# A convolution feeding a multiplicative FFN: block 3 transposed by DMA, and the first quarter of block 4 stored and transposed ahead of the rest

## The chip, the cores and the metric

The kernel runs on one core of a Trainium2 chip. The metric is device time in microseconds (us), one execution at a time; the profile is of one execution. The engines are named as the profile names them: PE (matmuls), ACT, DVE, POOL, and SP, which here only issues DMAs.

## The reference

A causal depthwise convolution with 7 taps per head (the softmax of `weight`, 8 heads of 24 channels), then a feed-forward block whose two input products are multiplied element by element and which has two linear layers behind that.

```python
w = softmax(weight, axis=-1)                          # 8 x 7
x_pad = concat([zeros(8, 6, 192), x], axis=1)         # x: 8 x 3904 x 192
t = einsum('hk,bskhg->bshg', w, windows(x_pad, 7))    # -> 31232 x 192
a, b = t @ w1, t @ w2                                 # 192 x 1024 each
out = ((a * b) @ w3) @ w_out                          # 1024 x 1024, 1024 x 192
```

## The kernel before

The 31232 tokens are handled as two streams of 15616 (`NS = 2`) in the two halves of the partitions. A stream is cut into windows of 58 tokens (64 rows with the 6 rows of padding), and the 272 windows are grouped into blocks of 10, 8, 10, 8, six of 36, and 20 windows. A *round* R is 512 tokens of both streams, so blocks 0 to 3 (2088 tokens) cover rounds 0 to 3 (2048 tokens), and block 4 (windows 36 to 71) covers rounds 4 to 7.

- `load_x(b)` brings a block's windows in from POOL's DMA queue with a cast (L112). `zero(b)` (L501) then clears the padding of windows at the start of a sequence; POOL waits there for the load.
- `conv(b, h0, nh, evict)` is the convolution as matmuls with a band matrix (L278); ACT or DVE copies the result from PSUM into `convo` (L295).
- The second product needs no transposing, the first does: `xT` holds the convolved rows with channels on partitions, in a ring of four rounds. Blocks 0 to 3 get there on PE, `pe_transposes(b)` (L331, copied out by ACT, DVE, ACT at L343). Later blocks go to a DRAM tile `rows` with `store(b)` (L322, L316; two DMAs a piece, of 48 and of 10 partitions, issued by SP), and come back by `transposes(R)`, three DMA transposes of 512 rows x 128 channels (L351, SP). The counters `stored` and `sent` tell `send(last)` which rounds may go.
- `first_product(R, between)` runs eight steps `ft`; each has 2 x 6 matmuls (L378) into two of four pairs of PSUM banks; ACT copies one to `asb` (L384), DVE multiplies it with the other into `abT` (L385). `between` puts convolutions and PE transposes behind given steps.
- `second_product(R, r)` (L404, L409) multiplies `abT` by `W_sb` and stores the result (L416; from POOL's queue in the first group, from SP's later).
- `W_sb` is w3 @ w_out, made on the chip: `load_w3` copies w3 to DRAM in bf16 in two halves (L430) and brings it back transposed with 16 DMA transposes on SP (L433), eight for each half of its rows; `w3_product(jt)` (L440) is eight matmuls over `gt`, and jt 0 to 3 read the first half of `w3T`, jt 4 to 7 the second.
- `P(out=pace, in_=w3T...)` (L472) makes POOL wait for one of these transposes before it issues the loads of blocks 4 and 5.

The order is written out by hand. First come rounds 0 to 3, with block R+1 convolved and transposed by PE inside round R for R = 0, 1, 2. Then `w3_product`, then the second products of rounds 0 to 3 with the convolution of block 4 (three slots of heads) and of block 5 between them. Then groups of four rounds follow: four first products, eight second products with the next block's convolution.

```python
    first_product(0, {
        3: seq((conv, 1, 0, 4)),
        5: seq((conv, 1, 4, 4)),
        6: seq((pe_transposes, 1))})
    for R in (1, 2):
        first_product(R, {
            0: seq((conv, R + 1, 0, 4)),
            2: seq((conv, R + 1, 4, 4)),
            5: seq((pe_transposes, R + 1))})
    store(3, FIRST[4] - 1)
    first_product(3)
```

Every engine runs its instructions in order, and each DMA issued by SP first waits for the DMA that was issued eight before it.

Of the kernel before, what the change touches and what calls it, by code (L numbers as in the profile page):

```python
# [16 lines left out]
def kernel(  # L17
# [10 lines left out]
    nc = tc.nc  # L28
# [4 lines left out]
    DFF = moe_w1.shape[1]  # L33
    JT = DFF // 128
# [3 lines left out]
    TS = B * S // NS  # L38
    CH = 512
    NR = -(-TS // CH)  # L40
    GROUP = 4
    RING = GROUP * CH
    Q = 64
    ST = Q - PAD
    NP = D // Q
    WB = -(-S // ST)
    NWIN = (B // NS) * WB
    LAST = S - (WB - 1) * ST
    SIZES = [10, 8, 10, 8] + [36] * 6 + [20]
    assert sum(SIZES) == NWIN  # L50
    NB = len(SIZES)
    FIRST = [sum(SIZES[:b]) for b in range(NB)]
# [3 lines left out]
    def tok(i):  # L56
        return (i // WB) * S + (i % WB) * ST
# [26 lines left out]
    rows = dram.tile([TS, NP * NS * Q], BF16, name="rows")  # L84


    def halves_of(b):
        n = SIZES[b] // 2
        return [(FIRST[b], 2 * n)] if 2 * n <= MAXN else [(FIRST[b], n), (FIRST[b] + n, n)]
# [8 lines left out]
    def load_x(b, parts=(0, 1)):  # L98
        tiles = xb_of.setdefault(b, [])
        zeros_of = zero_rows.setdefault(b, [])  # L100
        for i0, n in [v for e, v in enumerate(halves_of(b)) if e in parts]:
            xb = work.tile([128, n, D], BF16, tag="xb", bufs=5, name="xb")
            w = 0
            while w < n:
                i = i0 + w
                m = min(n - w, WB - i % WB)
                at_end = i + m == NWIN
                if at_end:
                    m -= 1
                if m:  # L110
                    for r in range(NS):
                        nc.gpsimd.dma_start(out=xb[Q * r:Q * r + Q, w:w + m, :],  # L112
                                            in_=x_spans(r, i, m))
                if i % WB == 0:
                    zeros_of += [(xb, 0, w), (xb, 1, w)]
                w += m
                if at_end:
                    nc.gpsimd.memset(xb[Q:128, w, :], 0.0)
                    t = tok(NWIN - 1) - PAD
                    nc.gpsimd.dma_start(out=xb[0:Q, w, :], in_=x_rows[t:t + Q, :])  # L120
                    nc.gpsimd.dma_start(out=xb[Q:Q + PAD + LAST, w, :],
                                        in_=x_rows[TS + t:TS + t + PAD + LAST, :])
                    w += 1
            if len(halves_of(b)) == 1:
                tiles += [(xb, 0), (xb, SIZES[b] // 2)]
            else:
                tiles.append((xb, 0))
# [8 lines left out]
    pace = const.tile([1, 2], BF16)  # L136
# [31 lines left out]
    for p0 in (0, Q):  # L168
        nc.gpsimd.affine_select(  # L169
            out=diag[p0:p0 + Q], in_=ones[p0:p0 + Q].to_broadcast([Q, Q + PAD]),  # L170
# [3 lines left out]
    for r in range(NS):  # L174
        nc.gpsimd.dma_start(out=xb0[Q * r + PAD:Q * r + Q, 0, :],
                            in_=x_rows[r * TS:r * TS + ST, :])
# [13 lines left out]
    def warm(n, t=None):  # L190
# [16 lines left out]
        out=wall, in0=wall, in1=wmax.unsqueeze(2).to_broadcast([1, H, K]), op=ALU.subtract)  # L207
# [6 lines left out]
        out=wrow, in0=wall, in1=wsum.unsqueeze(2).to_broadcast([1, H, K]), op=ALU.mult)  # L214
# [80 lines left out]
            f[e % len(f)](out=dst, in_=part)  # L295
        drained(p)

    stored, sent = [0], [GROUP]

    def store(b, first=0, queue=nc.sync):  # L300
        stored[0] = tok(FIRST[b] + SIZES[b]) if b + 1 < NB else TS
        n = SIZES[b] // 2
        convo = convo_of[b]
        for c in range(2):
            w = 0
            while w < n:
                i = FIRST[b] + c * n + w
                if i < first:
                    w += 1
                    continue  # L310
                left = WB - 1 - i % WB
                src = convo[Q * c:Q * c + ST, w:w + max(1, min(n - w, left))]
                src = src.rearrange("s w k r g -> s w (k r g)")
                j0 = tok(i)
                if left == 0:
                    queue.dma_start(out=rows[j0:j0 + LAST, :], in_=src[0:LAST, 0, :])  # L316
                    w += 1
                    continue
                m = min(n - w, left)
                dst = rows[j0:j0 + ST * m, :].rearrange("(w s) c -> s w c", s=ST)  # L320
                for s0, s1 in ((0, 48), (48, ST)):
                    queue.dma_start(out=dst[s0:s1], in_=src[s0:s1])  # L322
                w += m

    def pe_transpose(b, k):
# [36 lines left out]
    def width(R):  # L362
        return min(CH, TS - R * CH)

    def first_product(R, between=None):
        N = width(R)
        ab = work.tile([128, JT, NS, CH], BF16, tag="abT", bufs=GROUP, name="abT")
        abT_of[R] = ab
        r0 = (R * CH) % RING
        for ft in range(JT):  # L370
            pq = []
            for i in range(2):
                q, p = banks()
                pq.append((q, p))
                for k in range(NP):
                    for r in range(NS):
                        rs = slice(Q * r, Q * r + Q)
                        nc.tensor.matmul(  # L378
                            p[:, r, 0:N], wd[i][rs, k, ft * 128:(ft + 1) * 128],
                            xT[k][rs, r0:r0 + N],  # L380
                            start=(k == 0), stop=(k == NP - 1))
            (qa, pa), (qb, pb) = pq
            asb = work.tile([128, NS, CH], BF16, tag="asb", bufs=3, name="asb")
            nc.scalar.copy(out=asb[:, :, 0:N], in_=pa[:, :, 0:N])  # L384
            nc.vector.tensor_tensor(out=ab[:, ft, :, 0:N], in0=asb[:, :, 0:N],  # L385
                                    in1=pb[:, :, 0:N], op=ALU.mult)
            drained(qa)
            drained(qb)
            if between and ft in between:
                between[ft]()  # L390
# [34 lines left out]
    w3T = const.tile([128, JT, DFF], BF16)  # L425
    w3rows = dram.tile([DFF, DFF], BF16, name="w3rows")

    def load_w3():
        for j in range(0, DFF, CH):
            nc.gpsimd.dma_start(out=w3rows[j:j + CH], in_=moe_w3[j:j + CH])  # L430
        for j in range(0, DFF, CH):
            for gt in range(JT):
                nc.sync.dma_start_transpose(  # L433
                    out=w3T[:, gt, j:j + CH],
                    in_=w3rows[j:j + CH, gt * 128:(gt + 1) * 128])

    def w3_product(jt):
        p, wps = banks()
# [7 lines left out]
    V, A, P = nc.vector.tensor_copy, nc.scalar.copy, nc.gpsimd.tensor_copy  # L446
# [22 lines left out]
            copy_w(part, i, f)  # L469
    load_w3()  # L470
    nc.gpsimd.dma_start(out=wo_b, in_=wor)
    P(out=pace, in_=w3T[0:1, 1, DFF - 2:DFF])  # L472
    load_x(4)
    load_x(5)

    def seq(*fs):
        def run():
            for f, *a in fs:
                f(*a)
        return run  # L480

    def send(last):
        while sent[0] <= min(last, NR - 1) and min((sent[0] + 1) * CH, TS) <= stored[0]:
            transposes(sent[0])
            sent[0] += 1
# [2 lines left out]
        3: seq((conv, 1, 0, 4)),  # L488
        5: seq((conv, 1, 4, 4)),
        6: seq((pe_transposes, 1))})  # L490
    for R in (1, 2):
        first_product(R, {
            0: seq((conv, R + 1, 0, 4)),
            2: seq((conv, R + 1, 4, 4)),
            5: seq((pe_transposes, R + 1))})
    store(3, FIRST[4] - 1)
    first_product(3)

    def zero(b):
        for xb, r, w in zero_rows.pop(b, []):  # L500
            nc.gpsimd.memset(xb[Q * r:Q * r + PAD, w, :], 0.0)  # L501

    def conv_heads(b, heads, f=(nc.vector.tensor_copy,)):
        for j, h in enumerate(heads):
            conv(b, h, 1, (f[j % len(f)],))
        if heads[-1] == H - 1:
            store(b)

    slots = (range(0, 3), range(3, 6), range(6, H))
    zero(4)  # L510
# [6 lines left out]
    for p, rounds in enumerate(groups):  # L517
        b = PROLOGUE_BLOCKS + p
        order = rounds[-1:] + rounds[:-1] if rounds[-1] == NR - 1 else rounds
        for j, R in enumerate(order if p else ()):  # L520
            first_product(R)
            send(R + GROUP)
            if j < 2 and b < NB:
                P(out=pace, in_=abT_of[R][0:1, JT - 1, 1, 0:2])  # L524
                load_x(b, (j,))
        if b < NB:
            zero(b)
        at = {1: [(b, slots[0])], 3: [(b, slots[1])], 5: [(b, slots[2])]}
        if p == 0:
            at = {0: [(4, slots[1], (V, A))], 1: [(4, slots[2], (V, A))],  # L530
                  3: at[1], 5: at[3], 6: at[5]}
        for i, (R, r) in enumerate((R, r) for R in rounds for r in range(NS)):
            second_product(R, r, R == NR - 1 and r == 1, nc.sync if p else nc.gpsimd)
            for c in at.get(i, ()) if b < NB else ():
                conv_heads(*c)
            if p == 0 and i == 1:
                send(2 * GROUP - 1)
# [31 lines left out]
```

## Time and profile before

| | |
|---|---|
| median of 3 runs | 529.07 us (528.61 to 530.71) |
| the profiled execution | 530.22 us, of which the span from first to last instruction is 528.3 us |
| PE busy | 516.0 us, 98% |
| DVE, ACT busy | 359.1 us (68%), 325.0 us (62%) |
| round 0 starts on PE | 10.6 us |
| `w3_product` starts on PE | 60.0 us |
| last second product of rounds 0 to 3 ends | 90.9 us |
| matmuls of round 4 without pauses from | 96.6 us |
| a group of four first products later on | 41.55 us |

The span is the time between the first and the last instruction of the profile; the execution's own time has about 1.9 us around it. The busy time of PE is modelled for pipelined matmuls. The chain of waits follows the work that ended last back through what released it.

### The profile page before, as it was taken

What the parts mean: (1) busy time and instruction counts of PE and PEld (TensorE: products, weight loads), DVE (VectorE), ACT (ScalarE), POOL (GpSimd) and SP (SyncE); (2) the same over time, 40 slices, a digit from 0 to 9 for tenths busy, and PEclk for the clock granted to TensorE, in tenths of its full rate; (3) what the DMA queues carried; (4) which work ended last, traced back from release to release, by engine and by line L of the source; (5) the groups of instructions that cost most, each with busy time, mean ns of one, the idle gap of its engine ahead of it and who ended that gap; (6) DMA issues with size and microseconds to landing.
All of it is one profiled execution on the core that took longest, in us unless ns stands there. A gap on an engine that the chain in (4) does not pass through costs nothing.

```text
span 528.3 us, 12785 instructions
## 1 busy us (share of the span) xinstructions
PE 516.0 (98%) x5464; PEld 342.1 (65%) x5464; DVE 359.1 (68%) x347; ACT 325.0 (62%) x411; POOL 55.5 (10%) x93
## 2 busy tenths in 40 slices
PE   7999998799999999999999999999999999999997
PEld 4555787355786557965579555795558945599667
DVE  6777645499655996559964699637994289921880
ACT  5888642377536775367753777437774377744762
POOL 8405112012000110001200020000200000000000
PEclk9999999799999999999999999999999999999999
DMA  9999969699548793487834889347783631024004
GB/s 128 202 153 142 188 130 206 164 168 136 94 136 195 114 121 66 144 186 113 118 83 131 177 119 109 91 138 175 90 67 91 170 97 41 17 91 150 2 1 150
DMA packets 133381, 64.59 MB, mean 122 GB/s; under 512 B 90234, under 2 KB 132620, under 8 KB 133260
## 3 DMA queue, kind: packets, MB, share of 16 engines
q1 hardware_dynamic: 94378, 44.10, 37.2%
q0 software_dynamic: 38800, 19.58, 30.7%
q8 instruction: 42, 0.69, 0.5%
q14 instruction: 15, 0.12, 0.1%
q10 hardware_dynamic: 146, 0.10, 0.1%
HBM read 33.25 MB, written 36.52 MB: 132 GB/s over the span
## 4 chain that ended last, share of the span: by engine, by line
PE 93%; DMA 2%; DVE 2%; ACT 2%; issue 0%; POOL 0%; SPq 0%; POOLq 0%; ACTq 0%
PE pairs L378 58%; PE pairs L404 31%; PE pairs L278 2%; DVE abT L385 2%; ACT asb L384 1%; DMA xT<-rows 1%; PE pairs L440 1%; DMA xb<-in_x_dram 1%; PE pairs L331 1%; POOL xb L165 0%; DVE convo L449 0%; ACT xT L449 0%; ACT xT L343 0%; POOL diag L169 0%; ACT convo L295 0%
## 5 line engine op out<-in xcount | busy, mean ns | idle before, releaser
L385 DVE TENSOR_TENSOR abT<-asb,pairs 128x1024 bf16<-128x1024 bf16 (+1 forms) x248 | 298.4, 1204 | 83.1 <-ACT asb L384 44.6
L378 PE MATMUL pairs<-xT,wd 64*128 64x512 bf16 (+1 forms) x2976 | 322.5, 374 | 5.8 <-DMA xT<-rows 4.8
L384 ACT CAST asb<-pairs 128x1024 bf16<-128x1024 f32 (+1 forms) x248 | 247.6, 998 | 75.8 <-PE pairs L378 73.6
L378 PEld LDWEIGHTS <-wd 64*128 64x128 bf16 x2976 | 164.5, 94 | 157.9 <-issue 8.0
L404 PEld LDWEIGHTS <-abT 128*128 128x128 bf16 x1952 | 159.6, 98 | 9.7 <-issue 9.7
L404 PE MATMUL pairs<-W_sb,abT 128*128 128x192 bf16 x1952 | 165.9, 246 | 0.0
L409 ACT COPY osb<-pairs 128x384 f32<-128x384 f32 x122 | 58.3, 478 | 115.8 <-PE pairs L404 115.8
L295 DVE CAST convo<-pairs 128x864 bf16<-128x864 f32 (+5 forms) x67 | 50.8, 814 | 67.3 <-PE pairs L278 67.3
L112 POOL DMA_DIRECT2D xb<-in_x_dram x40 | 30.9, 791 | 7.9 <-PE pairs L378 4.6
L524 POOL COPY pace<-abT 1x2 bf16<-1x2 bf16 x10 | 1.7, 174 | 247.9 <-DVE abT L385 247.9
L278 PE MATMUL pairs<-xb,Aband 64*64 64x432 bf16 (+3 forms) x352 | 16.6, 294 | 1.0 <-DMA xb<-in_x_dram 1.0
L278 PEld LDWEIGHTS <-Aband 64*64 64x64 bf16 x352 | 6.6, 105 | 7.9 <-issue 6.9
L416 POOL DMA_DIRECT2D out_dram<-osb x8 | 6.1, 758 | 26.8 <-ACT osb L409 26.8
L295 ACT CAST convo<-pairs 128x512 bf16<-128x512 f32 (+4 forms) x15 | 8.1, 584 | 0.3 <-PE pairs L278 0.2
L409 DVE COPY osb<-pairs 128x192 f32<-128x192 f32 x1 | 0.4, 358 | 11.1 <-PE pairs L404 11.1
L440 PEld LDWEIGHTS <-w3T 128*128 128x128 bf16 x64 | 5.2, 98 | 0.4 <-issue 0.4
L440 PE MATMUL pairs<-wo_b,w3T 128*128 128x192 bf16 x64 | 5.5, 246 | 0.0
L195 PE MATMUL pairs<-zeros 128*128 128x512 bf16 x8 | 3.7, 595 | 1.3 <-DVE zeros L145 1.3
L331 PE MATMUL pairs<-identw,convo 128*128 128x128 bf16 x54 | 4.2, 219 | 0.7 <-DVE convo L449 0.6
L331 PEld LDWEIGHTS <-convo 128*128 128x128 bf16 x54 | 3.2, 97 | 2.5 <-issue 1.5
L442 ACT CAST W_sb<-pairs 128x192 bf16<-128x192 f32 x8 | 2.6, 319 | 2.8 <-PE pairs L440 2.8
L501 POOL MEMSET xb<- 6x192 bf16 x6 | 1.5, 250 | 21.7 <-DMA xb<-in_x_dram 21.7
(51 smaller groups left out, 40.6 us busy)
## 6 DMA issues: line engine op xcount, KB each, us to landing
out_dram<-osb SPq DMA_DIRECT2D x52, 384.0 KB
xb<-in_x_dram POOLq DMA_DIRECT2D x18, 432.0 KB, 8.6
rows<-convo SPq DMA_DIRECT2D x9, 648.0 KB
out_dram<-osb POOLq DMA_DIRECT2D x8, 384.0 KB, 6.7
w3rows<-in_moe_w_dram POOLq DMA_DIRECT2D x2, 1024.0 KB, 11.1
xb<-in_x_dram POOLq DMA_DIRECT2D x6, 240.0 KB, 5.7
xT<-rows SPq DMA_TRANSPOSE x81
rows<-convo SPq DMA_DIRECT2D x9, 135.0 KB
```

Of the source, the lines that this page charges most:

```text
L112: nc.gpsimd.dma_start(out=xb[Q * r:Q * r + Q, w:w + m, :], in_=x_spans(r, i, m))
L195: nc.tensor.matmul(t[:, j % 2, :], zeros[:, 0:128], zeros, start=True, stop=True)
L278: nc.tensor.matmul(view(slice(Q * c, Q * c + Q), r)[:, :, j * G:(j + 1) * G], band_of(h, r), xb[Q * r:Q * r + Q, w0:w0 + n, h * G:(h + 1) ...
L295: f[e % len(f)](out=dst, in_=part)
L331: nc.tensor.transpose(out=tps[:, w, :], in_=convo[:, w, k].rearrange("p r g -> p (r g)"), identity=ident)
L378: nc.tensor.matmul(p[:, r, 0:N], wd[i][rs, k, ft * 128:(ft + 1) * 128], xT[k][rs, r0:r0 + N], start=(k == 0), stop=(k == NP - 1))
L384: nc.scalar.copy(out=asb[:, :, 0:N], in_=pa[:, :, 0:N])
L385: nc.vector.tensor_tensor(out=ab[:, ft, :, 0:N], in0=asb[:, :, 0:N], in1=pb[:, :, 0:N], op=ALU.mult)
L404: nc.tensor.matmul(ops[:, (g - g0) * D:(g - g0) * D + D], ab[:, jt, r, g * 128:(g + 1) * 128], W_sb[:, jt, :], start=(jt == 0), stop=(jt = ...
L409: f(out=osb[:, g0:g0 + per, :].rearrange("p g d -> p (g d)"), in_=ops[:, 0:per * D])
L416: queue.dma_start(out=out[t0:t0 + ng * 128, :].rearrange("(g p) d -> p g d", p=128), in_=osb)
L440: nc.tensor.matmul(wps[:, 0, 0:D], w3T[:, gt, jt * 128:(jt + 1) * 128], wo_b[:, gt, :], start=(gt == 0), stop=(gt == JT - 1))
```

## The change

Four things move.

1. In round 1 blocks 2 and 3 are both convolved, the second half of the heads of each evicted by DVE instead of ACT; block 2's PE transposes come behind step 6. Round 2 has nothing between its steps.
2. Block 3 is no longer transposed by PE. Windows 26 and 27 of block 2 and all of block 3 are stored to `rows`, and round 3's part of `xT` comes by three DMA transposes (`sent` starts at 3).
3. On SP the 16 transposes of w3 are split: five, then the six stores, three more, round 3's three, then the eight of the second half. POOL's `pace` now waits for the first transpose of the second half (the ninth), formerly for the second of it (the tenth).
4. Block 4's windows 36 to 44 are stored first, round 4's three transposes follow, and then windows 45 to 71 with seven stores; before, all of block 4 was stored ahead of round 4's transposes.

```diff
-    stored, sent = [0], [GROUP]
-
-    def store(b, first=0, queue=nc.sync):
-        stored[0] = tok(FIRST[b] + SIZES[b]) if b + 1 < NB else TS
+    stored, sent = [0], [GROUP - 1]
+
+    def store(b, first=0, last=NWIN):
         n = SIZES[b] // 2
+        last = min(last, FIRST[b] + 2 * n)
+        stored[0] = tok(last) if last < NWIN else TS
...
-        for j in range(0, DFF, CH):
-            for gt in range(JT):
-                nc.sync.dma_start_transpose(
-                    out=w3T[:, gt, j:j + CH],
-                    in_=w3rows[j:j + CH, gt * 128:(gt + 1) * 128])
+
+    def w3_transposes(j, gts):
+        for gt in gts:
+            nc.sync.dma_start_transpose(
+                out=w3T[:, gt, j:j + CH], in_=w3rows[j:j + CH, gt * 128:(gt + 1) * 128])
...
-    P(out=pace, in_=w3T[0:1, 1, DFF - 2:DFF])
-    load_x(4)
-    load_x(5)
+    w3_transposes(0, range(5))
...
+    def need(R):
+        return next(i for i in range(NWIN) if tok(i) >= (R + 1) * CH)
...
-    for R in (1, 2):
-        first_product(R, {
-            0: seq((conv, R + 1, 0, 4)),
-            2: seq((conv, R + 1, 4, 4)),
-            5: seq((pe_transposes, R + 1))})
-    store(3, FIRST[4] - 1)
+    first_product(1, {
+        0: seq((conv, 2, 0, 4)),
+        1: seq((conv, 2, 4, 4, (V,))),
+        3: seq((conv, 3, 0, 4)),
+        4: seq((conv, 3, 4, 4, (V,))),
+        6: seq((pe_transposes, 2))})
+    store(2, need(GROUP - 2) - 1)
+    store(3)
+    w3_transposes(0, range(5, JT))
+    send(GROUP - 1)
+    w3_transposes(CH, range(JT))
+    first_product(2)
+    P(out=pace, in_=w3T[0:1, 0, DFF - 2:DFF])
+    load_x(4)
+    load_x(5)
     first_product(3)
...
         if heads[-1] == H - 1:
-            store(b)
+            store(b) if first is None else (store(b, last=first), send(NR), store(b, first))
...
-            at = {0: [(4, slots[1], (V, A))], 1: [(4, slots[2], (V, A))],
+            at = {0: [(4, slots[1], (V, A))], 1: [(4, slots[2], (V, A), need(GROUP))],
```

The built program shows the same order on each engine's queue: PE loses the 12 transposes of block 3, DVE gains four copies that ACT loses, ACT also loses two copies and DVE one of block 3's PE transposes, and SP gains four stores of blocks 2 and 3, two of block 4, and three DMA transposes.

More of the change, by code (lines that the diff above doesn't have):

```diff
@@ L296, in conv @@
         drained(p)
-    stored, sent = [0], [GROUP]
-    def store(b, first=0, queue=nc.sync):
-        stored[0] = tok(FIRST[b] + SIZES[b]) if b + 1 < NB else TS
+    stored, sent = [0], [GROUP - 1]
+    def store(b, first=0, last=NWIN):
         n = SIZES[b] // 2
+        last = min(last, FIRST[b] + 2 * n)
+        stored[0] = tok(last) if last < NWIN else TS
         convo = convo_of[b]
         for c in range(2):
[L305 to L314, printed above, removed]
-                if left == 0:
[L316 to L322, printed above, removed]
+            i0 = FIRST[b] + c * n
+            w, end = max(0, first - i0), min(n, last - i0)
+            while w < end:
+                left = WB - 1 - (i0 + w) % WB
+                m = min(end - w, max(1, left))
+                src = convo[Q * c:Q * c + ST, w:w + m].rearrange("s w k r g -> s w (k r g)")
+                j0 = tok(i0 + w)
+                if left == 0:
+                    nc.sync.dma_start(out=rows[j0:j0 + LAST, :], in_=src[0:LAST, 0, :])
+                else:
+                    dst = rows[j0:j0 + ST * m, :].rearrange("(w s) c -> s w c", s=ST)
+                    for s0, s1 in ((0, 48), (48, ST)):
+                        nc.sync.dma_start(out=dst[s0:s1], in_=src[s0:s1])
                 w += m
@@ L501, in zero, with conv_heads @@
             nc.gpsimd.memset(xb[Q * r:Q * r + PAD, w, :], 0.0)
-    def conv_heads(b, heads, f=(nc.vector.tensor_copy,)):
+    def conv_heads(b, heads, f=(nc.vector.tensor_copy,), first=None):
         for j, h in enumerate(heads):
```

## Prediction

> **What bounds the kernel now.** I read the busy row of the page first, then the chain of waits in order of time, then SP's and POOL's timelines of the first 145 us, and last a table of windows around the two places that the change touches.
>
> ```profile
> PE 516.0 (98%) x5464; PEld 342.1 (65%) x5464; DVE 359.1 (68%) x347; ACT 325.0 (62%) x411; POOL 55.5 (10%) x93
> ```
>
> PE is busy nearly throughout, so a gain must come from work taken off PE or from one of its few pauses. In the chain (start, length, what):
>
> ```profile
> 46.79 13.27 PE pairs L378 x120
> 60.06 5.39 PE pairs L440 x64
> 65.44 0.67 PE pairs L278 x12
> ...
> 90.88 0.12 SPq L351
> 91.00 0.04 issue
> 91.04 5.54 DMA xT<-rows
> 96.58 0.04 issue
> 96.62 43.09 PE pairs L378 x380
> ...
> 163.09 41.55 PE pairs L378 x384
> ```
>
> The large pause is at 90.88: PE has nothing to do until round 4's third transpose lands at 96.58. Rounds 4 to 7 end at 139.72; a group takes 41.55 undisturbed, so it would have begun at 139.72 - 41.55 = 98.17. The pause costs 98.17 - 90.88 = 7.29 us. Part of that is clock (first the stretch, its length and PE's busy time; the last three figures are granted clock, DMA share and GB/s):
>
> ```profile
> 90.00:93.00 3.00, 0.87 (x11) 0.64 (x8) 0.01 (x1) 0.59 (x2) 0.75 (x1) 1.00 0.55 77
> 93.00:97.00 4.00, 1.38 (x6) 0.34 (x8) 0.00 (x0) 0.00 (x0) 0.00 (x0) 0.59 1.17 293
> 97.00:101.00 4.00, 4.00 (x24) 1.77 (x22) 1.25 (x2) 2.02 (x2) 0.00 (x0) 0.56 0.44 98
> ```
>
> Waiting alone is 96.62 - 90.88 = 5.74, so the halved clock behind it costs about 1.55. The second place shows no pause yet: SP's queue (start, length, what), and then POOL's loads, which wait for a w3 transpose.
>
> ```profile
> 26.66 23.70 SPq L433 DMA_TRANSPOSE w3T<-w3rows  x16
> 50.45 30.00 SPq L322 DMA_DIRECT2D rows<-convo  x6
> 80.49 2.22 SPq L316 DMA_DIRECT2D rows<-convo  x1
> 82.76 3.61 SPq L322 DMA_DIRECT2D rows<-convo  x2
> 86.54 18.42 SPq L351 DMA_TRANSPOSE xT<-rows  x12
> ```
>
> ```profile
> 42.05 0.17 POOL L472 COPY pace<-w3T 1x2 bf16<-1x2 bf16 x1 [22.66 <-DMA w3T<-w3rows]
> 42.18 6.23 POOL L112 DMA_DIRECT2D xb<-in_x_dram  x8
> 59.32 0.25 POOL L501 MEMSET xb<- 6x192 bf16 x1 [0.25 <-DMA xb<-in_x_dram]
> ```
>
> A w3 transpose takes SP 1.30 us to issue. The landings that the trace records are, for the 10th to the 16th: 41.99, 43.31, 47.42, 52.27, 54.12, 55.98, 57.96. Up to the 11th it is 2.7 us from issue to landing. From the 12th, when POOL's loads flow, they land 1.85 apart after a hole of 4.9. The last is only 2.0 ahead of L440 at 59.99.
>
> **Round 4, at the end of the group.** SP issues the seven stores from 73.76 (`convo` complete) to 86.41, all 36 windows, and the transposes begin at 86.54. Afterwards 9 windows go first. The 18-window pair issued at 73.76 and 74.14 had landed by 83.7, 10 us; a quarter of the block's bytes, half of that pair, takes 5 to 7.4. With everything 3.4 later (below), the first stores go at 77.2 and have landed at 82.2 to 84.6. Three transposes at 1.30 to 2.2 each, landing 2.7 to 5.54 behind their issue, put the third in place at 87.5 to 94.5. PE ends its second products at 90.88 + 3.4 = 94.3 and needs the third 0.4 later. So the whole 7.29 goes, with a margin of 0.2 to 7.2.
>
> **Rounds 1 to 3 on PE.** Out go 12 PE transposes with their bank waits: matmul starts of round 2 show 44.94 + 0.65 before and 46.73 behind them, 1.14, and 0.15 more on the next step: 1.29 us, with 1.24 of ACT and 0.39 of DVE. The four convolution halves stay at 0.55 to 0.64 each. DVE takes four copies; by its rows of 0.45 for 288, 0.74 for 576 and 1.06 for 864 elements these are 0.48, 0.81, 0.42 and 0.68, 2.4 us, so round 1 is 8 x 1.22 + 0.45 + 2.4 = 12.6 on DVE against 8 x 1.295 + 4 x 0.58 + 1.29 = 14.0 on PE. PE still covers DVE, but with both convolutions in a round the four bank pairs wait for copies more often. The gain is between 0 and 1.29; I take 0.6, so that L440 would begin at 59.3.
>
> **SP's queue ahead of w3.** Five transposes, as before, end at 33.5. Six stores at 0.34 to 0.53 follow; the last four wait for block 3's copies, and the second half of its heads is copied by DVE behind round 1's fifth step, at about 35.2 (23.7, five steps of 1.295, three to four halves, and DVE's product in hand). SP is at 37.2. Three w3 transposes: 41.1. Round 3's transposes wait until the stores have landed: 10 windows, 0.45 MB, behind the fifth transpose (landed 37.5); the 36 windows issued at 105.05 took 12.0 us to the last landing, so 3.3 here plus some 1.5: 42.3. Three transposes: SP at 46.2, the third lands at 47.7; round 3 starts at 48.8 and is not held (1.1 us of cover; if that is gone, PE only waits earlier for what it waits for below). The ninth w3 transpose is issued at 46.2 and lands at 48.9. POOL's loads start behind it: 6.9 us later than at 42.05.
>
> **A new wait in `w3_product`.** Relative to the loads everything repeats, except that seven transposes are behind `pace` and not six: the 16th came 57.96 - 41.99 = 15.97 behind the one awaited, one more at 1.85 makes 17.8, so 48.9 + 17.8 = 66.7. jt 0 to 3 need only the first half and end at 59.3 + 2.7 = 62.0. jt 4 stops at its last `gt` until 66.7; 25 matmuls at 0.084 remain: L278 begins at 68.8 instead of 65.44, 3.4 later, and the 0.6 is swallowed. Block 4's loads ended with the memset 17.3 behind `pace`: 66.3 now, hidden behind L440. Bounds: if the queue only shifts by its extra issues (6 x 0.45 + 3 x 1.30 = 6.6) the 16th lands at 64.6, +1.3; if the six stores take the 10 us of 73.76, the loss is near +7. I take 3.4, since nothing from POOL runs beside these stores, as at 105.05.
>
> **Sum.** -7.29 + 3.4 = -3.9. The profiled execution had 530.22 (span 528.3), so 526.3 by its own time; the median of the three runs is 1.15 below, so 529.07 - 3.9 = 525.2.
>
> **Rivals.**
>
> *The clock falls in the new wait too.* PE has 4 us with a few single matmuls in it; at 90.88 it was halved after 2.8 us of that sort. The price is the 1.55 from above: 526.8. For it: the gaps are alike. Against: the halving comes at fixed marks 3.4 us apart in the records (88.75 and 6.83 us long stretches), and a gap of 4.4 need not fill one.
> The Trainium skill, TensorE: Matmul & The Clock Gate, Part 1, says that the clock drops to half after an idle window of about 3.4 us that runs free of the program; it speaks against this change, as it would charge the new gap in some runs. The trace agrees with it at 93.7.
>
> *The transposes are not held up by the loads.* If the last seven land at issue pace, 48.9 + 7 x 1.30 = 58.0, L440 isn't held and ends at 64.7. Then block 4's memset at 66.5 releases L278, +1.1: -7.29 + 1.1 = -6.2, 522.9. Against it stand the landings 47.42 to 57.96.
> This is how it would go by the Trainium skill, DMA: Bandwidth & Descriptors, Queues, rings and completion order: each DMA engine alternates between the queues that have work, a packet at a time. The hole of 4.9 us ahead of 52.27 disagrees.
>
> *Slower: round 5 waits in round 4's place.* Seven stores and then round 5's transposes stand behind round 4's on SP. PE wants round 5 at 94.3 + 10.4 + 0.4 = 105.1. SP is through with round 4's transposes at 86.1 to 91.2. The issue of seven such stores took 8.1 us at 159.62; the seven at 73.76, beside POOL's output stores, took 12.65. Round 5's third transpose lands 5.3 to 9.9 behind them: 99.5 to 113.7. At the far end PE waits 8.6 and the clock costs 1.55: -3.9 + 10.1 = +6.2, 535.3. It decides from 2.4 us of wait (with the clock), a landing at 107.5. For it: SP issued slowly as long as POOL's outputs ran, and they run beside these stores too. Against: 27 windows are three quarters of the 12.65, 9.5 us, and the outputs end at about 99.4, so the middle is 88.6 + 9.5 + 6.5 = 104.6, just in time. A landing between 105.1 and 107.5 gives 525 to 529.
>
> *Round 4 is still late.* If PE isn't delayed by w3 and the first stores and transposes take their far ends (94.5 - 3.4 = 91.1), PE at 90.88 + 0.4 meets them; the change does what it says there in either case. It has no chance of its own.
>
> **How the numbers follow.** About 0.5%, 2.6 us, is what a measurement of this kernel can tell from no change. Forecast (-3.9, from -1.5 to -6): 0.34, nine tenths of it faster. Clock in the new wait (-2.3): 0.19, half of it faster. No hold-up (-6.2): 0.10. Round 5 a little late (-3.5 to 0): 0.15, a fifth of it faster. Round 5 late enough to lose: 0.22, nine tenths of it slower by over 0.5%, since three long estimates hang on this one queue. Faster: 0.31 + 0.09 + 0.10 + 0.03 = 0.53; slower: 0.20; the rest, 0.27, is within 0.5%. The range goes from just under the case without hold-up, 522.0, to 531.0, a third of the way into the losing case (525.2 + 3.9 = 529.1 to 535.3), which leaves out some 0.13 above and 0.05 below.
>
> **What would show it.** Right: PE's pause at round 4 gone, granted clock 1.00 there; L440 with a pause of some 4 us ended by w3T; `pace` at 48 to 50; L278's first convolution of block 4 near 68.8. Wrong: L440 running through (then 523), a pause at L378 for round 3 or round 5 ended by xT, or round 4 still waiting.

## The result and the profile after

| | before | changed |
|---|---|---|
| median of 20 runs | 529.81 us (528.61 to 531.15) | 527.27 us (525.18 to 528.57) |
| ratio, 95% interval | | 0.9948 (0.9936 to 0.9959) |
| span of the profiled execution | 528.3 us | 525.6 us |

The change gains 2.5 us by the medians, 0.5%, and the interval of the ratio is clear of 1; 3.9 were forecast (525.2 in the range 522.0 to 531.0). In the changed kernel L436 is `w3_product` (L440 before), L374 the first products (L378), L347 the transposes of `xT` (L351), L430 those of w3 (L433), L318 the stores (L322), L400 the second products (L404), L500 `pace` (L472).

The chain of waits of the changed kernel:

```profile
55.76 10.60 DMA w3T<-w3rows
66.36 0.05 issue
66.41 3.44 PE pairs L436 x25
69.85 1.07 PE pairs L278 x11
...
92.93 2.75 PE pairs L400 x32
95.68 41.55 PE pairs L374 x384
```

The pause at round 4 is gone: second products end at 95.68 and the next group runs its 41.55 from there. The chain now has a DMA elsewhere, w3's last transpose, issued at 55.76 and landed at 66.36. So 95.68 - 90.88 = 4.80 us were lost ahead of round 4, and the 7.29 behind it were saved: -2.5.

PE around the new wait (start, length, what, and what ended the idle time before it):

```profile
59.24 3.31 PE L436 MATMUL pairs<-wo_b,w3T 128*128 128x192 bf16 x38
64.77 0.26 PE L436 MATMUL pairs<-wo_b,w3T 128*128 128x192 bf16 x1 [2.21 <-DMA w3T<-w3rows]
66.41 3.44 PE L436 MATMUL pairs<-wo_b,w3T 128*128 128x192 bf16 x25 [1.39 <-DMA w3T<-w3rows]
```

38 of the 64 matmuls run, one more waits for w3's 15th transpose, and the last `gt` of jt 4 for the 16th. The 25 matmuls behind it take 3.44 us; 64 took 5.39 before, so 25 would take 2.1. The table of windows shows why (the last three figures: granted clock, DMA share, GB/s):

```profile
62.00:67.00 5.00, 1.40 (x16) 1.02 (x14) 0.00 (x0) 0.62 (x2) 0.23 (x1) 1.00 1.37 139
67.00:71.00 4.00, 4.00 (x34) 2.89 (x33) 0.45 (x1) 1.21 (x5) 0.27 (x2) 0.57 1.60 192
92.00:96.00 4.00, 4.00 (x50) 3.16 (x49) 2.46 (x3) 1.25 (x3) 0.75 (x1) 1.00 0.98 229
```

The clock falls behind the new gap and not at round 4, where PE is now busy throughout. SP's queue, and POOL's:

```profile
33.63 3.33 SPq L318 DMA_DIRECT2D rows<-convo  x6
37.17 3.82 SPq L430 DMA_TRANSPOSE w3T<-w3rows  x3
41.23 4.71 SPq L347 DMA_TRANSPOSE xT<-rows  x3
45.99 12.16 SPq L430 DMA_TRANSPOSE w3T<-w3rows  x8
78.57 0.77 SPq L318 DMA_DIRECT2D rows<-convo  x2
83.95 4.10 SPq L347 DMA_TRANSPOSE xT<-rows  x3
...
98.36 12.58 SPq L347 DMA_TRANSPOSE xT<-rows  x9
```

```profile
48.70 0.17 POOL L500 COPY pace<-w3T 1x2 bf16<-1x2 bf16 x1 [29.32 <-DMA w3T<-w3rows]
48.83 7.07 POOL L112 DMA_DIRECT2D xb<-in_x_dram  x9
59.87 0.86 POOL L112 DMA_DIRECT2D xb<-in_x_dram  x1 [3.97 <-DMA xb<-in_x_dram]
66.77 0.63 POOL L507 MEMSET xb<- 6x192 bf16 x2 [6.04 <-DMA xb<-in_x_dram]
```

Round 4's transposes go 5.4 us behind the first store, and the other seven stores behind them. The six stores (3.33 us) and round 3's three transposes (4.71 us) now stand ahead of the ninth w3 transpose: it is issued at 45.99, which went at 37.99 before, and `pace` ends its wait at 48.70 in place of 42.05.

### The profile page after: what moved, and what is told of

Read it like the earlier page. It is cut to its first block, busy times and chain, and to the rows that moved or that the text cites. A ratio compares the mean times of both kernels' runs of the same rounds, so it can differ in the third digit from the quotient of the medians.

```text
span 525.6 us, 12773 instructions
## 1 busy us (share of the span) xinstructions
PE 514.5 (98%) x5452; PEld 341.5 (65%) x5452; DVE 360.7 (69%) x350; ACT 322.4 (61%) x405; POOL 55.4 (11%) x93
## 4 chain that ended last, share of the span: by engine, by line
PE 90%; DMA 3%; SPq 2%; ACT 2%; DVE 1%; issue 1%; POOL 0%; POOLq 0%; ACTq 0%
PE pairs L374 55%; PE pairs L400 31%; PE pairs L278 3%; DMA w3T<-w3rows 2%; SPq L430 2%; ACT asb L380 1%; DVE abT L381 1%; DMA xb<-in_x_dram 1%; PE pairs L436 1%; DVE convo L295 0%; POOL xb L165 0%; PE pairs L327 0%; ACT xT L339 0%; ACT convo L295 0%; DVE convo L445 0%
## 5 line engine op out<-in xcount | busy, mean ns | idle before, releaser
L374 PE MATMUL pairs<-xT,wd 64*128 64x512 bf16 (+1 forms) x2976 | 320.3, 373 | 1.2 <-DVE convo L295 0.3
L374 PEld LDWEIGHTS <-wd 64*128 64x128 bf16 x2976 | 163.4, 94 | 152.5 <-issue 3.9
L400 PEld LDWEIGHTS <-abT 128*128 128x128 bf16 x1952 | 159.6, 98 | 9.9 <-issue 9.9
L400 PE MATMUL pairs<-W_sb,abT 128*128 128x192 bf16 x1952 | 165.9, 246 | 0.0
L295 DVE CAST convo<-pairs 128x864 bf16<-128x864 f32 (+6 forms) x71 | 53.0, 803 | 72.8 <-PE pairs L278 67.9
L278 PE MATMUL pairs<-xb,Aband 64*64 64x432 bf16 (+3 forms) x352 | 17.0, 300 | 1.0 <-DMA xb<-in_x_dram 1.0
L278 PEld LDWEIGHTS <-Aband 64*64 64x64 bf16 x352 | 6.7, 107 | 8.2 <-issue 7.4
L436 PE MATMUL pairs<-wo_b,w3T 128*128 128x192 bf16 x64 | 7.0, 276 | 3.6 <-DMA w3T<-w3rows 3.6
L436 PEld LDWEIGHTS <-w3T 128*128 128x128 bf16 x64 | 6.2, 110 | 4.5 <-DMA w3T<-w3rows 4.0
L295 ACT CAST convo<-pairs 128x512 bf16<-128x512 f32 (+4 forms) x11 | 6.2, 605 | 1.1 <-PE pairs L278 1.0
L162 POOL DMA_DIRECT2D wd<-in_moe_w_dram x6 | 3.8, 641 | 0.0
L327 PE MATMUL pairs<-identw,convo 128*128 128x128 bf16 x42 | 3.1, 219 | 0.6 <-DVE convo L445 0.6
```

The lines of the kernel that those rows point to most:

```text
L162: nc.gpsimd.dma_start(out=wd[i][0:Q, :, cs], in_=w_rows[i][:, :, cs])
L278: nc.tensor.matmul(view(slice(Q * c, Q * c + Q), r)[:, :, j * G:(j + 1) * G], band_of(h, r), xb[Q * r:Q * r + Q, w0:w0 + n, h * G:(h + 1) ...
L374: nc.tensor.matmul(p[:, r, 0:N], wd[i][rs, k, ft * 128:(ft + 1) * 128], xT[k][rs, r0:r0 + N], start=(k == 0), stop=(k == NP - 1))
L400: nc.tensor.matmul(ops[:, (g - g0) * D:(g - g0) * D + D], ab[:, jt, r, g * 128:(g + 1) * 128], W_sb[:, jt, :], start=(jt == 0), stop=(jt = ...
L436: nc.tensor.matmul(wps[:, 0, 0:D], w3T[:, gt, jt * 128:(jt + 1) * 128], wo_b[:, gt, :], start=(gt == 0), stop=(gt == JT - 1))
```

## The experiments

Diffs are against the changed kernel unless another is named. Two questions: does the split of block 4's store alone carry the gain, and what makes the loss ahead of round 4? My theory was a queue on SP that is longer by nine DMAs ahead of w3's second half, then transposes held up by POOL's loads, then the clock.

**The split alone.** The prologue of before, with the split:

```diff
-    stored, sent = [0], [GROUP - 1]
+    stored, sent = [0], [GROUP]
-    w3_transposes(0, range(5))
+    w3_transposes(0, range(JT))
+    w3_transposes(CH, range(JT))
+    P(out=pace, in_=w3T[0:1, 1, DFF - 2:DFF])
+    load_x(4)
+    load_x(5)
...
+    for R in (1, 2):
+        first_product(R, {
+            0: seq((conv, R + 1, 0, 4)),
+            2: seq((conv, R + 1, 4, 4)),
+            5: seq((pe_transposes, R + 1))})
+    store(3, FIRST[4] - 1)
```

> The prologue of before, and only block 4's store split. Theory: the split alone removes the pause at round 4. The first stores go at 73.8 as before, and with the 12.0 us that the changed kernel took from its first store (78.57) to the landing of round 4's third transpose (90.57) that lands at 85.8, ahead of PE at 90.9; round 5's lands at 99.4 (25.6 us behind, as 104.16 in the changed kernel), ahead of 101.7. The whole 7.3 us goes and nothing is lost in w3: 522.5 if before is 529.8. Rival: the pause went because PE comes 4.8 us later to round 4; then 2.5 us are gained at most: 527.3.

Measured: 523.2 us (523.05 to 523.32), ratio 0.9863 (0.984 to 0.9887). Its SP queue and chain:

```profile
79.25 3.84 SPq L347 DMA_TRANSPOSE xT<-rows  x3
```

```profile
88.24 2.75 PE pairs L400 x32
90.99 41.55 PE pairs L374 x384
```

PE arrives at 90.99, as early as before, and doesn't wait: round 4's third transpose landed at 85.0 and round 5's at 99.0. So the split alone removes the whole pause; PE's later arrival isn't needed for it. By the median this is also the fastest version of all.

**All but the split.**

```diff
-1: [(4, slots[2], (V, A), need(GROUP))]
+1: [(4, slots[2], (V, A))]
```

> The changed kernel with block 4 stored whole again, so only its first half (blocks 2 and 3 in round 1, block 3 by DMA, w3's transposes split). Theory: L278 comes 4.8 us later by the wait in w3 and the clock behind it, the stores of block 4 move with it, and the pause at round 4 keeps its 7.3: 529.8 + 4.8 = 534.6. Rival: the later arrival at round 4 eats part of the pause: 529 to 532. If the first half costs nothing by itself: 529.8.

Measured: 535.27 us (531.51 to 537.88), ratio 1.0085 (1.0056 to 1.0113). Chain:

```profile
94.14 2.76 PE pairs L400 x32
96.90 0.24 SPq L347
97.14 0.04 issue
97.19 6.29 DMA xT<-rows
103.48 0.04 issue
103.52 44.12 PE pairs L374 x380
```

The other changes by themselves cost 5 us of median, and the pause follows PE to its later place. The profiled execution is the slowest of the eight; its pause with the clock behind it cost 103.52 + 44.12 - 41.55 - 96.90 = 9.2. The two parts add up: -7.1 and +4.95 give -2.2, and the whole change measured -2.5.

**No gap for the clock.** `warm(18)` issues 18 matmuls on a tile of zeros where PE would wait.

```diff
     for jt in range(JT):
+        if jt == JT // 2:
+            warm(18)
         w3_product(jt)
```

> The changed kernel with 18 matmuls on a tile of zeros (3.9 us of PE) between w3_product's jt 3 and jt 4, where PE waits. Theory: of the 4.8 us, 1.7 are the halved clock behind the gap; PE stays busy, the clock stays at 1.00, the 25 matmuls behind the last landing take 2.1 us in place of 3.44 and block 4's first convolution 0.67 in place of 1.07: 527.3 - 1.7 = 525.6. Rival: they are slow for another reason (late landings, banks): 527.3 or a little more.

Measured: 526.51 us (525.64 to 527.72), ratio 0.9924 (0.9898 to 0.995), 0.8 under the changed kernel by medians and 1.3 by ratios. The runs of the two overlap, so the profile carries the argument. PE:

```profile
62.48 4.05 PE L195 MATMUL pairs<-zeros 128*128 128x512 bf16 x18
66.36 2.81 PE L436 MATMUL pairs<-wo_b,w3T 128*128 128x192 bf16 x32
69.10 0.74 PE L278 MATMUL pairs<-xb,Aband 64*64 64x432 bf16 x12
```

Granted clock is 1.00 in that stretch, 32 matmuls take 2.81 us where 25 took 3.44, and block 4's first convolution takes 0.74 in place of 1.14. The slow matmuls were the clock's. Less came out than the 1.7 expected because the zeros stand ahead of jt 4: 32 of its matmuls follow them and not 25, 0.6 us. Second products end at 94.59, 1.09 earlier than in the changed kernel, near the 1.14 that 1.74 - 0.6 gives.

**Without the loads beside the transposes.**

```diff
-    P(out=pace, in_=w3T[0:1, 0, DFF - 2:DFF])
+    P(out=pace, in_=w3T[0:1, JT - 1, DFF - 2:DFF])
```

> The changed kernel with POOL's loads of blocks 4 and 5 behind the last of w3's 16 transposes, not the ninth. Theory: the last seven are late because the loads run beside them; without these they land at issue pace, the 16th at 58.5 to 59.5 in place of 66.4, and w3_product runs through from 59.2 to 64.6. The loads begin at 59 and block 4's memset comes 14 to 17.3 later, so L278 begins at 73 to 76.5, 3 to 6.5 later than in the changed kernel: 530.5 to 534. Rival: they are late by themselves (the transposes behind round 3's are slow): the 16th lands at 64 or later, w3_product is held as it was, and L278 begins behind 80: above 537.

Measured: 531.46 us (528.76 to 532.65), ratio 1.0018 (0.9998 to 1.0038): no faster than the kernel before. POOL's timeline, and PE's:

```profile
59.57 0.17 POOL L500 COPY pace<-w3T 1x2 bf16<-1x2 bf16 x1 [39.42 <-DMA w3T<-w3rows]
```

```profile
59.56 5.45 PE L436 MATMUL pairs<-wo_b,w3T 128*128 128x192 bf16 x64
...
72.34 1.66 PE L278 MATMUL pairs<-xb,Aband 64*64 64x432 bf16 x10 [3.98 <-POOL xb L507]
```

The ninth to the 16th land 48.70, 49.80, 51.10, 52.41, 53.66, 55.09, 56.39, 59.51: issue pace but for the last, which is 3.1 behind the 15th with none of POOL's loads beside it. In the changed kernel they land 48.64, 49.95, 54.26, 57.73, 59.72, 61.58, 64.72, 66.36. The loads hold them, and without them `w3_product` runs through; but then PE waits for block 4's loads, and the record of the clock is at half for 6.83 us from 69.59 on. The Trainium skill (DMA: Bandwidth & Descriptors, Queues, rings and completion order) has each DMA engine take a packet from each queue in turn. I would now read an even slowing of the transposes from that, an inference, and not the landings at issue pace that I took from it in the prediction; the record has two holes of 4.31 and 3.47 us and steps of 1.6 to 3.1 behind them. What in the queues makes the holes I haven't shown.

**The dense round by itself.** The split alone, with both convolutions in round 1 and DVE's copies, block 3 still transposed by PE (against the split alone):

```diff
-    for R in (1, 2):
-        first_product(R, {
-            0: seq((conv, R + 1, 0, 4)),
-            2: seq((conv, R + 1, 4, 4)),
-            5: seq((pe_transposes, R + 1))})
+    first_product(1, {
+        0: seq((conv, 2, 0, 4)),
+        1: seq((conv, 2, 4, 4, (V,))),
+        3: seq((conv, 3, 0, 4)),
+        4: seq((conv, 3, 4, 4, (V,))),
+        6: seq((pe_transposes, 2))})
+    first_product(2, {5: seq((pe_transposes, 3))})
```

> The split-only kernel (523.2, 0.986 of before) with blocks 2 and 3 both convolved in round 1 and DVE's four copies, as in the changed kernel, but block 3 still transposed by PE, in round 2: no stores and no transposes for round 3, SP's queue ahead of w3 as before. Theory: the loss of the changed kernel's first half comes from SP's queue alone; w3's 16th lands at 58, L436 starts at 60.0 to 60.6 and is not held: 0.986 to 0.988 of before, 523 to 524. Rival: the dense round 1 (bank waits, DVE's copies) carries part of the loss: 525 or more.

Measured: 523.77 us (523.54 to 524.62), ratio 0.9894 (0.9881 to 0.9908). PE here, and then with the split alone:

```profile
22.88 2.82 PE L374 MATMUL pairs<-xT,wd 64*128 64x512 bf16 x24 [0.17 <-ACT xT L339]
...
61.06 5.45 PE L436 MATMUL pairs<-wo_b,w3T 128*128 128x192 bf16 x64
```

```profile
22.44 2.87 PE L374 MATMUL pairs<-xT,wd 64*128 64x512 bf16 x24
...
60.11 5.45 PE L436 MATMUL pairs<-wo_b,w3T 128*128 128x192 bf16 x64
```

From the last step of round 0 to L436 PE needs 61.06 - 22.88 = 38.18, against 60.11 - 22.44 = 37.67 with the split alone. The dense round costs 0.5 in these two profiles, and `w3_product` runs through. So the wait in `w3_product` comes with what this kernel leaves out, SP's longer queue and the loads that start later behind it; which of the nine DMAs costs how much wasn't tried one by one.

**Fewer transposes behind the loads.**

```diff
-    P(out=pace, in_=w3T[0:1, 0, DFF - 2:DFF])
+    P(out=pace, in_=w3T[0:1, 3, DFF - 2:DFF])
     load_x(4)
+    P(out=pace, in_=w3T[0:1, JT - 1, DFF - 2:DFF])
     load_x(5)
```

> The changed kernel with block 4's loads behind the 12th of w3's transposes (not the ninth) and block 5's behind the 16th. Theory: what counts is how many transposes are still out when the loads start. The 12th lands at 52.4 unheld; four are left, as behind the 12th of before minus two, so the 16th lands 12 later, 64.5, and block 4's loads 13 to 14 behind the 12th, 66.5, without block 5's beside them. L278 starts at about 67 to 67.5 in place of 69.85, with a smaller gap for the clock: 524 to 525.5, 0.989 to 0.991 of before. Rival: the hold is as long however few are out (the 16th at 66 or later): 527 or more.

Measured: 527.58 us (526.37 to 527.81), ratio 0.9959 (0.9946 to 0.9973): no gain over the changed kernel. PE:

```profile
64.77 2.24 PE L436 MATMUL pairs<-wo_b,w3T 128*128 128x192 bf16 x25 [1.40 <-DMA w3T<-w3rows]
66.94 0.37 PE L278 MATMUL pairs<-xb,Aband 64*64 64x432 bf16 x2
69.02 1.01 PE L278 MATMUL pairs<-xb,Aband 64*64 64x432 bf16 x10 [1.71 <-POOL xb L508]
```

The profiled run is the one of the five in which the clock didn't fall (526.45, mean granted clock 1.000; the others had 0.997). The transposes came as the theory said, the 16th at 64.73 for 64.5. Block 4's loads didn't: they landed at 68.78, 16 us behind the transpose awaited, and not 13 to 14. I had taken the 12.9 (72.47 - 59.57) that they needed with no transposes beside them. Transposes and loads hold up each other, and moving the start between them moves the wait from the one to the other.

**DVE for the second halves.** Against the split alone:

```diff
-            2: seq((conv, R + 1, 4, 4)),
+            2: seq((conv, R + 1, 4, 4, (V,))),
```

> The split-only kernel with the second half of the heads of blocks 2 and 3 evicted by DVE. Theory: ACT's copies behind each half cost PE about 0.2 us of bank wait each, DVE has the room: 0.2 to 0.4 less than the split-only kernel, 0.9855 of before, hardly to be told from it. Rival: DVE's product is what the banks wait for (L385 ended waits of L378 in the chain of before), so it gets later: 523.5 to 524.

Measured: 524.52 us (524.01 to 525.71), ratio 0.9908 (0.9895 to 0.9921): slower, as the rival had it, and by more than its 523.5 to 524. In its chain a convolution's copy on DVE stands ahead of PE:

```profile
28.85 1.10 issue
29.96 0.37 DVE convo L295
...
30.36 0.83 DVE convo L295
...
31.23 1.49 PE pairs L374 x12
```

The copies stand behind DVE's product, and the bank pair that PE wants next is free only at 31.2. The same copies stand in the changed kernel's chain at 28.67 to 29.90.

## Why the forecast was right in its way and 1.4 off

**Round 4** held. The third transpose lands at 90.57, 5.5 ahead of its use, inside the forecast margin of 0.2 to 7.2, and the kernel with the split alone gains 7.1 of the 7.29.

**Rounds 1 to 3** held: L436 begins at 59.24 in place of 59.99, 0.75 for the 0.6 taken, and the wait behind it swallows it.

**SP's queue and the wait in `w3_product`** held to 0.4 us: stores issued until 37.0 (forecast 37.2), the ninth transpose issued at 45.99 (46.2) and landed at 48.64 (48.9), the 16th landed at 66.36 (66.7). In part that is luck: round 3's transposes went at 41.23, as the stores had landed by 39.86 and held nothing (42.3 forecast), and then took 4.71 to issue for 3.9. Without the clock L278 would have begun at 66.41 + 2.1 = 68.5, 3.1 later than before for the 3.4 forecast. The hold-up, taken over from before's landings, repeated in its sum: 17.7 us between the ninth and the 16th, 17.8 forecast. Its steps didn't: one hole of 4.85 and one of 4.1 before, 4.31 and 3.47 now, and another of 3.14 ahead of the 15th.

**The clock** is the term that failed. The sum had 0 for it and the rival 1.55, with a chance of 0.19 against the forecast's 0.34. In the profiled execution it cost 1.74: 3.44 - 2.1 = 1.34 in L436 and 0.40 in the first convolution. In 17 of the 20 runs the mean granted clock was 0.993 to 0.997, and one stretch of 3.41 us at half takes 0.003 from the mean (1.7 of 525.6 us); where the stretch lies only the profiled run shows. The other three, at 1.000, took 525.18 to 525.20. That this is the forecast's 525.2 is chance, as the forecast stood on a median of 529.07 from three runs: from the 529.81 of 20 runs its 3.9 gives 525.9, and the rival's 2.3 gives 527.5, where 527.27 was measured. So the rival was the likelier of the two, and I had it the wrong way round. The reason that I gave, that a gap of 4.4 us need not fill one stretch of 3.4, is what was wrong: the record of the clock goes down at 67.23, and the 3.41 us ahead of that (63.82 on) held 1.08 us of matmuls, one at 64.77 and those from 66.41 on. The Trainium skill (TensorE: Matmul & The Clock Gate, Part 1) speaks of an idle window; here one with a third of its time in matmuls was idle enough.

**The other rivals.** No hold-up is refuted by the landings and by the kernel without loads beside them. Round 5 in round 4's place didn't come: its third transpose landed at 104.16 (forecast for the middle 104.6), PE needed it at 95.68 + 10.4 + 0.4 = 106.5, 2.3 later. In the kernel with the split alone it landed at 99.0 and was needed at 101.8.

## What to carry to other kernels

When a late transfer stalls PE, split the producer so that what is needed first is stored and fetched first; it cost nothing that shows here and was worth 7 us. Work that is moved off the busiest engine onto a queue pays with everything queued behind it: 1.3 us of PE transposes became 8 us on a queue whose last entries had 2 us to spare. A new wait next to PE should be priced with the clock behind it from the start, also if single matmuls stand in it.

## What the runs showed of the hardware

- DMA transposes issued 1.30 us apart land 1.1 to 1.4 apart with none of POOL's loads beside them, but for the last of eight, 3.1 behind the one ahead. In the changed kernel, once POOL's loads flow, two land 4.31 and 3.47 us behind the one ahead, the rest 1.6 to 3.1. The loads are slowed in turn: block 4's took 12.9 us with no transposes beside them and 16 to 18 beside four to seven.
- A gap need not be empty for the clock to fall. Counted in steps of 3.41 us from the changes in the record of the clock, a stretch with 1.08 us of matmuls was followed by half the clock in the changed kernel, and one with 1.12 in the kernel without the split. Stretches with 1.85 and 1.89 (loads in two parts) and 2.15 (changed kernel, the one ahead) were not. The changed kernel's pauses were 2.21 and 1.39 us, with one matmul between them. With matmuls on zeros in the gap the clock stayed at 1.00.
- The granted clock separates the runs of the changed kernel: 525.2 at 1.000, 526.1 to 528.6 below. It doesn't do so everywhere: with the 18 matmuls on zeros, runs at 1.000 took 525.7 to 527.0.
